# Other rows of a down-projection weight loaded apart, with 8 in place of 5 as the outermost dimension

## The chip, the cores and the metric

The kernel runs on one core of one Trainium2 chip. The metric is the time of one launch on the device in microseconds. Before the change it is 199.98 us (median of three runs, 199.91 to 200.15). A core has TensorE (PE; its weight loads are shown apart as PEld), VectorE (DVE), ScalarE (ACT), GpSimd (POOL) and SyncE (SP). Sixteen DMA engines move data between the chip's memory and the core's own memory, whose tiles have up to 128 partitions (rows) each.

## The reference

One token for each of 8 sequences passes a layer norm, then two branches that share the normalised `xn`, and the branches are multiplied:

```python
xn = _layernorm(x, axis=-1)                       # x: 8 x 1 x 512
s = _A_ref(xn, k_cache, v_cache, wq, wo)          # attention
g = _silu(_B_ref(xn, w_gate, w_up, w_down))       # gated unit
return x + s * g

# _A_ref: 32 query heads of 128, 8 key/value heads, the last 2048 of 8192 cached positions
# _B_ref:
g = xn @ w_gate; u = xn @ w_up                    # 512 x 1792 each
return (sigmoid(g) * u) @ w_down                  # 1792 x 512
```

All tensors are bf16. The caches are most of the traffic: the window of each sequence is 4 MB of keys and 4 MB of values, 67 MB in all. The weights wq, wo, w_gate, w_up and w_down add 4, 4, 1.75, 1.75 and 1.75 MB.

## The kernel before

Almost every load is issued from SP's queue (`q0`), in an order written out by hand: `later` puts a load on a list, and `pump` issues from the head of the list as long as the load's pool has a free buffer. There are two pools of large buffers, "k" with five and "v" with four; `free` gives a buffer back when its reader is done, and pumps. The order is: x and w_gate, w_up, the larger part of w_down, wq in two loads, the rest of w_down (`want_part`), then for 8 sequences x 2 halves of the heads a K tile and, three places later, a V tile of 2 MB each, and at last wo in five loads of 12, 8, 6, 4 and 2 rows per partition. SP carries out its instructions in order, so a load that has to wait for a buffer or for a semaphore holds up all that are behind it. Loads take turns on eight semaphores, and a load on a semaphore waits until the load before it on that semaphore has completed.

The work goes in this order. The layer norm and the transposes of `xn`; `hidden` (L291) multiplies by w_gate and w_up, with four column blocks of 448 side by side in the partitions of one PSUM tile; a sigmoid (L308), a product (L312) and a 32 x 32 block transpose on DVE (L320) give `hT_sb`, the hidden values with one of 14 rows per partition in each slice. The down projection (L348) multiplies slice by slice with the rows of w_down and ends in the gate `gg_sb` (L375). Then q (L385), and for each sequence the K tiles are transposed on TensorE (L481), copied (L486) and multiplied with q (L500); a softmax on ACT (L548); transposes of the weights (L571); the product with V (L597). The last lines multiply by wo (L719, L733), by the gate (L748) and add x (L750).

w_down has 1792 rows of 1 KB, 14 to a partition. Rows 1 to 13 of each partition are one load of 128 partitions (`wd_sb`, 13 KB per partition). Row 0 of all 128 partitions, 128 KB, goes elsewhere: `want_part` (L179) clears a tile of 64 partitions x 3 slots on POOL and fills it with three loads, whose source has an outermost dimension of 5, 5 and 4:

```python
PARTS = ((0, NA, 0, SX, 0, A), (Z, NA, 0, SX, SX * NA, A))     # A = 5, NA = 20, SX = 3, Z = 32
PARTS += ((Z + NA, P - 2 * SX * NA, 0, 1, 2 * SX * NA, 4),)
...
in_=src.rearrange("(y a) n -> a y n", a=a)[:, :, : SD * w.shape[1]],
```

As these rows lie in other partitions than the hidden values that belong to them, the kernel shifts the hidden values too: `sel_part` (L276 to L285), a 0/1 matrix made with seven copies, three matmuls (L327) and a copy (L335) put slice 0 of `hT_sb` into the partitions of `wd_part`. The down projection then is 13 matmuls with `wd_sb` and three with `wd_part`.

Of the kernel before, what the change touches and what calls it, by code (L numbers as in the profile page):

```python
# [10 lines left out]
def kernel(  # L11
# [13 lines left out]
    nc = tc.nc  # L25
    P = 128
    B, _, D = A_x.shape
    _, Hkv, Sk, Dh = A_k_cache.shape
# [3 lines left out]
    F = B_w_gate.shape[1]  # L32
    KT = D // P
    FT = F // P
# [14 lines left out]
    bf16 = mybir.dt.bfloat16  # L49
    f32 = mybir.dt.float32  # L50
    AF = mybir.ActivationFunctionType
    ALU = mybir.AluOpType
# [6 lines left out]
    vpool = ctx.enter_context(tc.tile_pool(name="vpool", bufs=4))  # L59
    ktpool = ctx.enter_context(tc.tile_pool(name="ktpool", bufs=3))  # L60
    ppool = ctx.enter_context(tc.tile_pool(name="ppool", bufs=2))
    consts = ctx.enter_context(tc.tile_pool(name="consts", bufs=1))
    work = ctx.enter_context(tc.tile_pool(name="work", bufs=1))
    small = ctx.enter_context(tc.tile_pool(name="small", bufs=2))
    ps_t = ctx.enter_context(
        tc.tile_pool(name="ps_t", bufs=4, space=bass.MemoryType.PSUM)
    )
# [13 lines left out]
    q0, q1 = nc.sync, nc.scalar  # L81
# [22 lines left out]
    weights = {}  # L104
    todo = []

    def later(tag, f):
        todo.append((tag, f))
# [7 lines left out]
    def free(tag):  # L116
        room[tag] += 1
        pump()

    def want_rows(name, w, tag, per, r0, r1):  # L120
        def f():
            t = load_rows(w, tag, per, r0, r1, name)
            for r in range(r0, r1):
                weights[(name, r)] = t[:, r - r0, :]

        later(tag, f)
# [13 lines left out]
    Z = 32  # L140
    S = Z // B
    NB = D // P
# [24 lines left out]

    A = 5  # L170
    SD = 1
    SX = 3
    HP = P // 2
    NA = 4 * A
    PARTS = ((0, NA, 0, SX, 0, A), (Z, NA, 0, SX, SX * NA, A))
    PARTS += ((Z + NA, P - 2 * SX * NA, 0, 1, 2 * SX * NA, 4),)
    d_room = []

    def want_part(w, per):  # L179
        def f():  # L180
            d = vpool.tile([HP, SX, SD, w.shape[1]], bf16, name="wd_part", tag="v")
            d_room.append(d)
            nc.gpsimd.memset(d[:], 0.0)
            for p0, n, x0, x1, s0, a in PARTS:
                m = n * (x1 - x0)
                src = w.rearrange("(y r) n -> y (r n)", r=per)[s0 : s0 + m]
                q0.dma_start(
                    out=d[p0 : p0 + n, x0:x1].rearrange("p x r n -> p (x r n)"),
                    in_=src.rearrange("(y a) n -> a y n", a=a)[:, :, : SD * w.shape[1]],
                )  # L190

        later("v", f)

    want_rows("wd_sb", B_w_down, "v", FT, SD, FT)
    for i in range(2):
        want_rows("wq_sb", A_wq, "k", KT, 2 * i, 2 * i + 2)
    want_part(B_w_down, FT)
    order = [(b, i) for b in range(B) for i in range(NQ)]
    AHEAD = 3
    for n in range(len(order) + AHEAD):  # L200
# [4 lines left out]
    for t0, t1 in ((0, 12), (12, KS), (KS, 26), (26, 30), (30, RT)):  # L205
# [4 lines left out]
    ident = consts.tile([P, P], bf16, name="ident")  # L210
# [6 lines left out]
        out=perm[:].rearrange("k (l p) -> k l p", l=G),  # L217
        in_=ident[:].rearrange("k (p l) -> k l p", l=G),
# [13 lines left out]
        out=rstd[:], in_=mv[:, 1:2], func=AF.Sqrt, bias=eps_t[:], scale=1.0  # L232
# [4 lines left out]
        out=xn_bf[:],  # L237
        in0=x_f[:],
# [7 lines left out]
    for kt in range(KT):  # L246
        nc.tensor.transpose(  # L247
            out=xnT_ps[:, kt, :],
            in_=xn_bf[:].rearrange("b (p kt) -> b kt p", kt=KT)[:, kt, :],
            identity=ident[:B, :B],  # L250
        )
    xnT_sb = work.tile([P, KT, Z], bf16, name="xnT_sb")
# [8 lines left out]
    for t in p_buf:  # L261
# [7 lines left out]
        out=own_q[:], in_=ident_f[:].rearrange("k (h q) -> k q h", q=NDQ), axis=AX.X  # L269
# [3 lines left out]
        out=sel_z[:], in_=ident_f[:].rearrange("k (j z) -> k z j", z=Z), axis=AX.X  # L273
    )

    sel_part = consts.tile([P, SX, HP], bf16, name="sel_part")  # L276
    nc.vector.memzero(sel_part[:])
    for p0, n, x0, x1, s0, a in PARTS:
        for x in range(x0, x1):
            nc.vector.tensor_copy(  # L280
                out=sel_part[:, x, p0 : p0 + n].rearrange("k (a e) -> k a e", a=a),
                in_=ident[:, s0 : s0 + n * (x1 - x0)].rearrange(
                    "k (e x a) -> k x a e", x=x1 - x0, a=a
                )[:, x - x0],
            )  # L285

    FC = F // NB

    def hidden(name):  # L291
        ps = ps_t.tile([P, FC], f32, name="h_ps", tag="t")
        for kt in range(KT):
            for j in range(NB):
                nc.tensor.matmul(  # L295
                    ps[Z * j : Z * (j + 1), :],
                    lhsT=xnT_sb[:, kt, :],
                    rhs=weights[(name, kt)][:, j * FC : (j + 1) * FC],
                    start=(kt == 0),
                    stop=(kt == KT - 1),  # L300
                    tile_position=(0, Z * j),
                    skip_group_check=True,
                )
        return ps

    g_ps = hidden("wg_sb")
    sig = ktpool.tile([P, CU * P // 2], f32, name="sig", tag="kT")
    nc.scalar.activation(out=sig[:, :FC], in_=g_ps[:], func=AF.Sigmoid)  # L308
    free("v")
    u_ps = hidden("wu_sb")  # L310
    h_sb = work.tile([P, FT, Z], bf16, name="h_sb")
    nc.vector.tensor_tensor(  # L312
        out=h_sb[:].rearrange("k t p -> k p t"),
        in0=sig[:, :FC].rearrange("k (p t) -> k p t", t=FT),
        in1=u_ps[:].rearrange("k (p t) -> k p t", t=FT),
        op=ALU.mult,
    )
    free("v")
    hT_sb = work.tile([P, FT, Z], bf16, name="hT_sb")
    nc.vector.transpose(  # L320
        out=hT_sb[:].rearrange("k t z -> k (t z)"),
        in_=h_sb[:].rearrange("k t p -> k (t p)"),
    )

    hP_ps = ps_t.tile([HP, SX, SD * Z], f32, name="hP_ps", tag="t")
    for x in range(SX):
        nc.tensor.matmul(  # L327
            hP_ps[:, x, :],
            lhsT=sel_part[:, x, :],
            rhs=hT_sb[:, :SD, :].rearrange("p t z -> p (t z)"),  # L330
            start=True,
            stop=True,
        )
    hP_sb = work.tile([HP, SX, SD * Z], bf16, name="hP_sb")
    nc.vector.tensor_copy(out=hP_sb[:], in_=hP_ps[:])  # L335
    down = [(hT_sb[:, t, :], weights[("wd_sb", t)]) for t in range(SD, FT)]
    for x in range(SX):
        top = max(p0 + n for p0, n, x0, x1, _, _ in PARTS if x0 <= x < x1)
        down += [
            (hP_sb[:top, x, Z * r : Z * (r + 1)], d_room[0][:top, x, r, :])  # L340
            for r in range(SD)
        ]


    w_ps = ps_s.tile([P, D], f32, name="w_ps", tag="s")
    for t, (h, w) in enumerate(down):
        j = t % NB
        nc.tensor.matmul(  # L348
            w_ps[Z * j : Z * (j + 1), :],
            lhsT=h,  # L350
            rhs=w,
            start=(t < NB),
            stop=(t >= len(down) - NB),
            tile_position=(0, Z * j),
            skip_group_check=True,
# [4 lines left out]
    for j in range(NB):  # L360
        nc.tensor.matmul(  # L361
            b_ps[Z * j : Z * (j + 1), :],
            lhsT=sel_z[:],
            rhs=w_sb[:, 0, j * P : (j + 1) * P],
            start=True,
            stop=True,
            tile_position=(0, Z * j),
            skip_group_check=True,
        )
    sigb = work.tile([P, P], f32, name="sigb")  # L370
    nc.scalar.activation(out=sigb[:], in_=b_ps[:], func=AF.Sigmoid)  # L371
    free("v")
    free("v")
    gg_sb = work.tile([P, P], f32, name="gg_sb")
    nc.vector.tensor_tensor(out=gg_sb[:], in0=sigb[:], in1=b_ps[:], op=ALU.mult)  # L375
# [5 lines left out]
    for kt in range(KT):  # L381
        for x in range(Hkv // JQ):
            for j in range(JQ):
# [3 lines left out]
                    lhsT=xnT_sb[:, kt, :],  # L387
                    rhs=weights[("wq_sb", kt)][:, g * rep * Dh : (g + 1) * rep * Dh],
                    start=(kt == 0),
                    stop=(kt == KT - 1),  # L390
                    tile_position=(0, Z * j),
                    skip_group_check=True,
# [3 lines left out]
    for x in range(Hkv // JQ):  # L396
        src = q_ps[x][:].rearrange("k (r d) -> k r d", r=rep)
# [4 lines left out]
    for x in range(Hkv // JQ):  # L402
        for r in range(rep):
            nc.tensor.transpose(  # L404
                out=qT_ps[:, x, r, :], in_=q_bf[:, x, r, :], identity=ident[:]
            )
        nc.vector.tensor_copy(
            out=qm_sb[:, :, x * JQ : (x + 1) * JQ, M0 : M0 + rep],
            in_=qT_ps[:, x].rearrange("d r (j z) -> d z j r", z=Z)[:, ::S],
# [11 lines left out]
    for i in range(NQ):  # L421
        nc.vector.tensor_copy(
            out=turn_rows[:].rearrange("k (i j l r) -> k i j l r", i=NQ, j=NJ, l=G)[
                :, i
            ],
            in_=ident[:].rearrange("k (l j i r) -> k i j l r", i=NQ, j=NJ, l=G)[:, i],
        )
        nc.vector.reduce_sum(
            out=sel_den[:, i * Hh : (i + 1) * Hh].rearrange("k (l r) -> k l r", l=G),
            in_=ident_f[:].rearrange("k (l j i r) -> k i l r j", l=G, j=NJ, i=NQ)[:, i],  # L430
            axis=AX.X,
        )
    for e in range(2):
        nc.vector.reduce_sum(
            out=sel_out[:, e, :].rearrange("k (i h) -> k i h", i=NQ),
            in_=ident_f[:].rearrange(
                "k (i m e h) -> k e i h m", i=NQ, m=NJ // 2, e=2
            )[:, e],
# [9 lines left out]
        out=sel_res[:],  # L448
        in0=sel_out[:, 0, :].unsqueeze(2).to_broadcast([P, Hq, NDQ]),
        in1=sel_out[:, 1, :].unsqueeze(2).to_broadcast([P, Hq, NDQ]),  # L450
        op=ALU.add,
# [3 lines left out]
        out=sel_sum[:], in_=sel_den[:].unsqueeze(2).to_broadcast([P, Hq, NDQ])  # L455
# [261 lines left out]
    for t in range(KS):  # L717
        j = t % NB
# [69 lines left out]
```

## Time and profile before

| what | value |
|---|---|
| time, median of 3 runs | 199.98 us (199.91 to 200.15) |
| profiled execution, span from first to last instruction | 198.0 us |
| around the span (199.98 - 198.0) | 2.0 us |
| PE, DVE, ACT busy in the span | 155.6, 122.6, 37.7 us |
| bytes read from memory | 81.02 MB, 409 GB/s over the span |
| last load's landing, start of the stores | 193.74 us, 194.87 us |

The page gives the busy time of each engine, a row of 40 slices of the span with the busy share of the DMA engines in tenths, and the queues with the share of the sixteen engines' time that their packets took. q1 is SP's queue, q10 is ACT's; q8 and q14 bring instructions. The waits list who stood idle and what ended it: "PE w_ps L348 <- DMA wd_part" is time in which the matmul of line 348 waited for that load, followed by the sum, the number of times and the longest. In the timeline, a bracket holds the idle time before an instruction and what ended it. The trace behind the page also holds every DMA packet with its start, length, size and queue, and the time of every semaphore update.

### The profile page before, as it was taken

What the parts mean: (1) busy time and instruction counts of PE and PEld (TensorE: products, weight loads), DVE (VectorE), ACT (ScalarE), POOL (GpSimd) and SP (SyncE); (2) the same over time, 40 slices, a digit from 0 to 9 for tenths busy, and PEclk for the clock granted to TensorE, in tenths of its full rate; (3) what the DMA queues carried; (4) which work ended last, traced back from release to release, by engine and by line L of the source; (5) the groups of instructions that cost most, each with busy time, mean ns of one, the idle gap of its engine ahead of it and who ended that gap; (6) DMA issues with size and microseconds to landing.
All of it is one profiled execution on the core that took longest, in us unless ns stands there. A gap on an engine that the chain in (4) does not pass through costs nothing.

```text
span 198.0 us, 4774 instructions
## 1 busy us (share of the span) xinstructions
PE 155.6 (79%) x2133; PEld 105.6 (53%) x2133; DVE 122.6 (62%) x234; ACT 37.7 (19%) x91; POOL 2.7 (1%) x11
## 2 busy tenths in 40 slices
PE   0434038999979999999798869996999997888552
PEld 0111014877766677656565646674667665566421
DVE  3773001999978679758675927686767874852301
ACT  3300011000620520150024000600060033082010
POOL 5000000000000000000000000000000000000000
PEclk9999999999999999999999979997899999999985
DMA  6999999999999999999999999999999999999980
GB/s 209 446 430 434 426 425 427 434 440 429 424 420 430 430 427 437 430 430 420 430 427 425 427 440 430 422 434 424 424 430 440 420 430 437 427 420 425 420 336 10
DMA packets 6441, 81.32 MB, mean 411 GB/s; under 512 B 782, under 2 KB 918, under 8 KB 1558
## 3 DMA queue, kind: packets, MB, share of 16 engines
q1 hardware_dynamic: 6224, 80.10, 95.0%
q10 hardware_dynamic: 198, 0.93, 1.4%
q8 instruction: 16, 0.26, 0.5%
q14 instruction: 3, 0.02, 0.0%
HBM read 81.02 MB, written 0.01 MB: 409 GB/s over the span
## 4 chain that ended last, share of the span: by engine, by line
DMA 57%; PE 36%; ACT 3%; DVE 1%; SPq 1%; issue 1%
DMA k_sb<-in_A_k_cache_dram 32%; PE kT_ps L481 19%; DMA wo_sb<-in_A_wo_dram 11%; DMA wd_part<-in_B_w_down_dram 10%; PE o_ps L597 6%; PE s_ps L500 5%; DMA wg_sb<-in_B_w_gate_dram 3%; ACT p_buf L548 2%; PE pT_ps L571 2%; PE q_ps L385 1%; SPq L99 1%; ACT L548 1%; PE qT_ps L404 1%; PE fin_ps L733 1%; PE b_ps L361 0%
## 5 line engine op out<-in xcount | busy, mean ns | idle before, releaser
L486 DVE COPY kT_sb<-kT_ps 128x1024 bf16<-128x1024 bf16 x128 | 85.4, 687 | 30.2 <-PE kT_ps L481 29.5
L481 PE MATMUL kT_ps<-perm,k_sb 128*128 128x128 bf16 x1024 | 78.0, 225 | 8.2 <-DMA k_sb<-in_A_k_cache_dram 8.2
L481 PEld LDWEIGHTS <-k_sb 128*128 128x128 bf16 x1024 | 61.1, 101 | 28.0 <-issue 16.7
L597 PE MATMUL o_ps<-v_sb,pT_sb 128*32 128x256 bf16 x512 | 40.3, 279 | 1.2 <-DVE o_sb L618 0.9
L597 PEld LDWEIGHTS <-pT_sb 128*32 128x32 bf16 x512 | 22.1, 97 | 10.3 <-issue 3.8
L500 PE MATMUL s_ps<-kT_sb,qm_sb 128*32 128x512 bf16 x256 | 26.0, 396 | 0.7 <-DVE kT_sb L486 0.7
L548 ACT ACTIVATE p_buf<-s_ps,nb 32x512 bf16<-32x512 f32 x32 | 21.8, 680 | 0.5
L541 ACT COPY nb<-m_ps 128x1 f32<-128x1 f32 x8 | 1.3, 160 | 88.3 <-PE m_ps L535 88.3
L571 PE MATMUL pT_ps<-turn_rows,p_buf 128*128 128x128 bf16 x128 | 11.0, 230 | 1.5 <-ACT p_buf L548 1.5
L564 DVE COPY pT_sb<-pT_ps 128x1024 bf16<-128x1024 bf16 x14 | 9.6, 687 | 3.9 <-PE pT_ps L571 3.9
L571 PEld LDWEIGHTS <-p_buf 128*128 128x128 bf16 x128 | 9.4, 151 | 3.4 <-ACT p_buf L548 2.1
L500 PEld LDWEIGHTS <-qm_sb 128*32 128x32 bf16 x256 | 6.6, 93 | 7.7 <-issue 1.4
L613 ACT ACTIVATE o_odd<-o_ps,own_col 128x128 f32<-128x128 f32 x8 | 2.9, 368 | 26.8 <-PE o_ps L597 26.7
L375 DVE TENSOR_TENSOR gg_sb<-sigb,b_ps 128x128 f32<-128x128 f32 x1 | 0.3, 289 | 12.2 <-ACT sigb L371 12.2
L348 PE MATMUL w_ps<-wd_part,hP_sb 52*32 52x512 bf16 (+1 forms) x3 | 0.6, 597 | 8.3 <-DMA wd_part<-in_B_w_down_dram 8.3
L548 ACT ACTIVATION_READ_ACCUMULATOR p_buf<-s_ps,nb 32x1 f32 x32 | 5.9, 184 | 0.0
L515 DVE TENSOR_REDUCE st<-s_ps 128x1 f32<-128x512 f32 x8 | 5.5, 682 | 0.5 <-PE s_ps L500 0.5
L348 PEld LDWEIGHTS <-hP_sb 52*32 52x32 bf16 (+1 forms) x3 | 0.1, 98 | 9.2 <-issue 9.2
L247 PE MATMUL xnT_ps<-ident,xn_bf 8*128 8x8 bf16 x4 | 0.3, 174 | 5.8 <-DVE xn_bf L236 5.8
L640 DVE SCALAR_TENSOR_TENSOR own<-m_ps,inv,own_q 128x128 f32<-128x128 f32 x8 | 2.8, 345 | 3.1 <-PE m_ps L631 3.1
L618 DVE SCALAR_TENSOR_TENSOR o_sb<-o_ps,own_col,o_odd 128x128 f32<-128x128 f32 x8 | 2.7, 341 | 3.1 <-ACT o_odd L613 3.1
L295 PE MATMUL h_ps<-wu_sb,xnT_sb 128*32 128x448 bf16 x16 | 1.7, 572 | 3.4 <-DMA wu_sb<-in_B_w_up_dram 3.4
(80 smaller groups left out, 67.1 us busy)
## 6 DMA issues: line engine op xcount, KB each, us to landing
k_sb<-in_A_k_cache_dram SPq DMA_DIRECT2D x16, 2048.0 KB, 29.9
v_sb<-in_A_v_cache_dram SPq DMA_DIRECT2D x16, 2048.0 KB, 27.2
wq_sb<-in_A_wq_dram SPq DMA_DIRECT2D x2, 2048.0 KB, 19.9
wu_sb<-in_B_w_up_dram SPq DMA_DIRECT2D x1, 1792.0 KB, 10.3
wd_sb<-in_B_w_down_dram SPq DMA_DIRECT2D x1, 1664.0 KB, 13.8
wo_sb<-in_A_wo_dram SPq DMA_DIRECT2D x1, 1536.0 KB
wo_sb<-in_A_wo_dram SPq DMA_DIRECT2D x1, 1024.0 KB, 20.1
wg_sb<-in_B_w_gate_dram ACTq DMA_DIRECT2D x1, 896.0 KB
```

The source lines that it names most:

```text
L99: q0.dma_start(out=t[:], in_=w.rearrange("(p r) n -> p r n", r=per)[:, r0:r1, :])
L481: nc.tensor.transpose(out=kT_ps[:, c, :], in_=k_sb[:, j * CU + h * CH + c, :], identity=perm[:],)
L486: nc.vector.tensor_copy(out=kT[(b, u)][:, h * CH : (h + 1) * CH, :], in_=kT_ps[:])
L500: nc.tensor.matmul(s_ps[b][NR * l : NR * (l + 1), :], lhsT=qm_sb[:, b, i * G + l, o : o + Z], rhs=t[:, :, PG * l : PG * (l + 1)], start=(u ...
L515: nc.vector.reduce_max(out=st[b][:], in_=s_ps[b][:], axis=AX.X)
L548: nc.scalar.activation(out=p_buf[b % 2][rows, :, l, :], in_=s[rows, :].rearrange("k (c p) -> k p c", p=PG), func=AF.Exp, bias=nb[rows, :], ...
L564: copy(out=pT[b][:, h * CH : (h + 1) * CH, :], in_=pT_ps.pop(h)[:])
L571: nc.tensor.transpose(out=pT_ps[h][:, c, :], in_=p_buf[b % 2][:, :, :, h * CH + c].rearrange("k p l -> k (p l)"), identity=turn_rows[:],)
L597: nc.tensor.matmul(o_ps[rows, b % 2, :].rearrange("k (e d) -> k e d", e=2), lhsT=pT[b][:, c, rows], rhs=v[:, m, c], start=(c == 0), stop=( ...
L613: nc.scalar.mul(out=o_odd[:], in_=o_ps[:, b % 2, Dh:], mul=own_col[:, 1:2])
L618: nc.vector.scalar_tensor_tensor(out=o_of[b // 2][:, b % 2, :], in0=o_ps[:, b % 2, :Dh], scalar=own_col[:, 0:1], in1=o_odd[:], op0=ALU.mul ...
L640: nc.vector.scalar_tensor_tensor(out=own[:], in0=m_ps[:, b % 2, P : 2 * P].rearrange("p (q t) -> p q t", q=NDQ), scalar=inv[y][:, b % 2 : ...
```

## The change

All 128 partitions now hold 12 rows of w_down each (rows 0 to 1535), one load of 12 KB per partition. The last 256 rows go, four to a partition, into partitions 0 to 63 of the same tile, in slots 12 to 15, with two loads of 32 partitions. Their source is written with 8 as its outermost dimension and 4 as the next, so that destination partition 4 a + p takes its 4 KB from block 8 p + a. All three loads are issued one after another, ahead of wq. The separate tile, its memset, its place in the "v" pool, `sel_part`, the three shifting matmuls and their copy are gone.

The hidden values are now computed where they are needed: `hidden` multiplies, beside four column blocks of 384 for the first 12 rows, two blocks of 128 for the last four, into the same PSUM tile; sigmoid, product and transpose are each done in two pieces, one over 128 partitions and one over 64. The down projection has 12 matmuls over 128 partitions and four over 64.

```diff
-    A = 5
-    SD = 1
-    SX = 3
     HP = P // 2
-    NA = 4 * A
-    PARTS = ((0, NA, 0, SX, 0, A), (Z, NA, 0, SX, SX * NA, A))
-    PARTS += ((Z + NA, P - 2 * SX * NA, 0, 1, 2 * SX * NA, 4),)
-    d_room = []
-
-    def want_part(w, per):
-        def f():
-            d = vpool.tile([HP, SX, SD, w.shape[1]], bf16, name="wd_part", tag="v")
-            d_room.append(d)
-            nc.gpsimd.memset(d[:], 0.0)
-            for p0, n, x0, x1, s0, a in PARTS:
...
-        later("v", f)
-
-    want_rows("wd_sb", B_w_down, "v", FT, SD, FT)
+    F0 = FT - 2
+    FX = 4
+    FR = F0 + FX
+    NE = 8
+
+    def want_down():
+        t = vpool.tile([P, FR, D], bf16, name="wd_sb", tag="v")
+        q0.dma_start(
+            out=t[:, :F0, :],
+            in_=B_w_down[: P * F0].rearrange("(p r) n -> p r n", r=F0),
+        )
+        for j in range(HP // Z):
+            f0 = P * F0 + j * Z * FX
+            q0.dma_start(
+                out=t[j * Z : (j + 1) * Z, F0:, :].rearrange("p r n -> p (r n)"),
+                in_=B_w_down[f0 : f0 + Z * FX].rearrange(
+                    "(p a r) n -> a p (r n)", a=NE, r=FX
+                ),
+            )
+        for r in range(FR):
+            weights[("wd_sb", r)] = t[:, r, :] if r < F0 else t[:HP, r, :]
+
+    later("v", want_down)
     for i in range(2):
         want_rows("wq_sb", A_wq, "k", KT, 2 * i, 2 * i + 2)
-    want_part(B_w_down, FT)
...
-    sel_part = consts.tile([P, SX, HP], bf16, name="sel_part")
...
-    FC = F // NB
+    FC = Z * F0
+    FE = Z * FX
...
+                w = weights[(name, kt)]
+                cols = [(0, FC, j * FC)]
+                if j < HP // Z:
+                    cols.append((FC, FE, NB * FC + j * FE))
+                for at, n, f0 in cols:
+                    nc.tensor.matmul(
+                        ps[Z * j : Z * (j + 1), at : at + n],
+                        lhsT=xnT_sb[:, kt, :],
+                        rhs=w[:, f0 : f0 + n],
...
-    nc.scalar.activation(out=sig[:, :FC], in_=g_ps[:], func=AF.Sigmoid)
+    h_parts = ((P, 0, FC), (HP, FC, FC + FE))
+    for n, f0, f1 in h_parts:
+        nc.scalar.activation(out=sig[:n, f0:f1], in_=g_ps[:n, f0:f1], func=AF.Sigmoid)
...
+    nc.vector.tensor_tensor(
+        out=h_sb[:HP, F0:, :].rearrange("k t (a p) -> k p a t", a=NE),
+        in0=sig[:HP, FC : FC + FE].rearrange("k (p a t) -> k p a t", a=NE, t=FX),
+        in1=u_ps[:HP, FC : FC + FE].rearrange("k (p a t) -> k p a t", a=NE, t=FX),
+        op=ALU.mult,
+    )
...
-    hP_ps = ps_t.tile([HP, SX, SD * Z], f32, name="hP_ps", tag="t")
...
-    hP_sb = work.tile([HP, SX, SD * Z], bf16, name="hP_sb")
-    nc.vector.tensor_copy(out=hP_sb[:], in_=hP_ps[:])
...
+    for n, t0, t1 in ((P, 0, F0), (HP, F0, FR)):
+        nc.vector.transpose(
+            out=hT_sb[:n, t0:t1, :].rearrange("k t z -> k (t z)"),
+            in_=h_sb[:n, t0:t1, :].rearrange("k t p -> k (t p)"),
+        )
+    down = [
+        (hT_sb[: P if t < F0 else HP, t, :], weights[("wd_sb", t)]) for t in range(FR)
+    ]
...
     nc.scalar.activation(out=sigb[:], in_=b_ps[:], func=AF.Sigmoid)
-    free("v")
     free("v")
```

More of the change, by code (lines that the diff above doesn't have):

```diff
@@ L165 @@
     want_rows("wu_sb", B_w_up, "v", KT, 0, KT)
-    A = 5
-    SD = 1
-    SX = 3
     HP = P // 2
-    NA = 4 * A
-    PARTS = ((0, NA, 0, SX, 0, A), (Z, NA, 0, SX, SX * NA, A))
-    PARTS += ((Z + NA, P - 2 * SX * NA, 0, 1, 2 * SX * NA, 4),)
-    d_room = []
-    def want_part(w, per):
-        def f():
-            d = vpool.tile([HP, SX, SD, w.shape[1]], bf16, name="wd_part", tag="v")
-            d_room.append(d)
-            nc.gpsimd.memset(d[:], 0.0)
-            for p0, n, x0, x1, s0, a in PARTS:
[L185 to L190, printed above, removed]
-        later("v", f)
-    want_rows("wd_sb", B_w_down, "v", FT, SD, FT)
+    F0 = FT - 2
[19 more added lines that the diff above has]
+    later("v", want_down)
     for i in range(2):
         want_rows("wq_sb", A_wq, "k", KT, 2 * i, 2 * i + 2)
-    want_part(B_w_down, FT)
     order = [(b, i) for b in range(B) for i in range(NQ)]
@@ L274 @@
     )
-    sel_part = consts.tile([P, SX, HP], bf16, name="sel_part")
[L277 to L285, printed above, removed]
-    FC = F // NB
+    FC = Z * F0
+    FE = Z * FX
     def hidden(name):
-        ps = ps_t.tile([P, FC], f32, name="h_ps", tag="t")
+        ps = ps_t.tile([P, FC + FE], f32, name="h_ps", tag="t")
         for kt in range(KT):
             for j in range(NB):
[L295 to L303, printed above, removed]
+                w = weights[(name, kt)]
[7 more added lines that the diff above has]
+                        rhs=w[:, f0 : f0 + n],
+                        start=(kt == 0 and at == 0),
+                        stop=(kt == KT - 1),
+                        tile_position=(0, Z * j),
+                        skip_group_check=True,
+                    )
         return ps
@@ L307 @@
     sig = ktpool.tile([P, CU * P // 2], f32, name="sig", tag="kT")
-    nc.scalar.activation(out=sig[:, :FC], in_=g_ps[:], func=AF.Sigmoid)
+    h_parts = ((P, 0, FC), (HP, FC, FC + FE))
+    for n, f0, f1 in h_parts:
+        nc.scalar.activation(out=sig[:n, f0:f1], in_=g_ps[:n, f0:f1], func=AF.Sigmoid)
     free("v")
     u_ps = hidden("wu_sb")
-    h_sb = work.tile([P, FT, Z], bf16, name="h_sb")
+    h_sb = work.tile([P, FR, Z], bf16, name="h_sb")
+    hT_sb = work.tile([P, FR, Z], bf16, name="hT_sb")
     nc.vector.tensor_tensor(
-        out=h_sb[:].rearrange("k t p -> k p t"),
-        in0=sig[:, :FC].rearrange("k (p t) -> k p t", t=FT),
-        in1=u_ps[:].rearrange("k (p t) -> k p t", t=FT),
+        out=h_sb[:, :F0, :].rearrange("k t p -> k p t"),
+        in0=sig[:, :FC].rearrange("k (p t) -> k p t", t=F0),
+        in1=u_ps[:, :FC].rearrange("k (p t) -> k p t", t=F0),
+        op=ALU.mult,
[4 more added lines that the diff above has]
+        in1=u_ps[:HP, FC : FC + FE].rearrange("k (p a t) -> k p a t", a=NE, t=FX),
         op=ALU.mult,
@@ L318 @@
     free("v")
[L319 to L323, printed above, removed]
-    hP_ps = ps_t.tile([HP, SX, SD * Z], f32, name="hP_ps", tag="t")
[L326 to L332, printed above, removed]
-        )
-    hP_sb = work.tile([HP, SX, SD * Z], bf16, name="hP_sb")
-    nc.vector.tensor_copy(out=hP_sb[:], in_=hP_ps[:])
[L336 to L342, printed above, removed]
+    for n, t0, t1 in ((P, 0, F0), (HP, F0, FR)):
+        nc.vector.transpose(
+            out=hT_sb[:n, t0:t1, :].rearrange("k t z -> k (t z)"),
+            in_=h_sb[:n, t0:t1, :].rearrange("k t p -> k (t p)"),
+        )
+    down = [
+        (hT_sb[: P if t < F0 else HP, t, :], weights[("wd_sb", t)]) for t in range(FR)
+    ]
     w_ps = ps_s.tile([P, D], f32, name="w_ps", tag="s")
```

## The prediction

> **What bounds the kernel now.** I read the DMA rows of the page first, because the slices of that row never fall.
>
> ```profile
> span 198.0 us, 4774 instructions
> ...
> DMA  6999999999999999999999999999999999999980
> ...
> DMA packets 6441, 81.32 MB, mean 411 GB/s; under 512 B 782, under 2 KB 918, under 8 KB 1558
> ## 3 DMA queue, kind: packets, MB, share of 16 engines
> q1 hardware_dynamic: 6224, 80.10, 95.0%
> ...
> q8 instruction: 16, 0.26, 0.5%
> q14 instruction: 3, 0.02, 0.0%
> ```
>
> The reader is to see that the queue of SP alone fills 95.0% of sixteen DMA engines' time, and that instruction queues (q8, q14) use the same engines. Next the end of the timeline, and the last step of the chain of waits in order of time:
>
> ```profile
> 190.12 0.62 PE L719 MATMUL part_ps<-wo_sb,oP_sb 128*32 128x512 bf16 x8 [1.21 <-DMA wo_sb<-in_A_wo_dram]
> ...
> 193.17 1.01 PE L733 MATMUL fin_ps<-wo_sb,oP_sb 128*32 128x128 bf16 x24 [0.39 <-DMA wo_sb<-in_A_wo_dram]
> ...
> 194.23 0.29 DVE L748 TENSOR_TENSOR prod<-gg_sb,fin_ps 128x128 f32<-128x128 f32 x1 [6.20 <-PE fin_ps L733]
> ```
>
> ```profile
> 170.90 22.23 DMA wo_sb<-in_A_wo_dram
> 193.17 1.04 PE fin_ps L733 x23
> ```
>
> TensorE stands waiting for rows of wo that were issued 22 us before: the end is the landing of the last load (193.74 by its last semaphore update), plus a fixed 4.3 us. Last, the stage of the change:
>
> ```profile
> PE w_ps L348 <- DMA wd_part<-in_B_w_down_dram: 8.3, 1, 8.3
> ...
> SPq L187 <- DMA wg_sb<-in_B_w_gate_dram: 1.7, 2, 1.3
> ```
>
> ```profile
> L187 SPq DMA_DIRECT2D wd_part<-in_B_w_down_dram x3: 675/752/974, 5.4 to 7.6; - x3
> ```
>
> The 8.3 us wait looks like the prize. It is not: a core that is bound by its DMA engines cannot finish sooner because TensorE starts sooner.
>
> **The sixteen engines, one by one.** The trace keeps each DMA packet's start, length, size and queue, but not its engine. On a busy engine a packet starts 3 or 4 ns before the last one's recorded end (a 16 KB packet is recorded as 611 ns and the next starts after 607), so packets can be joined into chains. From 8.5 us to the end all join into sixteen chains without a gap over 40 ns. So every engine is busy all the time at one pace, and the kernel ends with the engine that has most to do. From an engine's first wu packet to its last packet:
> - three engines have nothing extra: 183.40 us; they end at 189.98, 190.29, 190.50.
> - eight have two 16 KB instruction fetches of q8 each: 186.23. A fetch costs its engine (186.23 - 183.40)/2 = 1.42 us. They end at 193.00, 193.15, 193.24, 193.27, 193.35, 193.35, 193.38, 193.40, and these set the end.
> - five have the 1 KB packets of wd_part (24 of them: 184.43). They end at 190.89, 191.70, 191.84, and, with one and two 8 KB fetches of q14, 192.18 and 193.05.
>
> So the old load put its lump on five engines that have no q8 fetch. The question is which eight engines the new lump meets. A load's completions show how many engines it used: the two 20-partition parts (5 outermost) gave five updates each, the third (4) four, x_bf (8 partitions) eight, a 128-partition load sixteen. The eight of x_bf are a sample of "8 outermost". Followed from their 1 KB packets at 1.7 to 2.9 us, they are the five with wd_part, one with nothing extra (ends 189.98), and two with fetches: the one ending at 193.24 (joined packet to packet) and the one ending at 193.15 (joined only by order: the five engines that finish x_bf first are taken for the five that start wg first). By that, at least one engine that is already among the latest gets more.
>
> **The change part by part.** *Loads of w_down.* Packets of 13 KB come every 494 ns, of 12 KB (first wo load) every 456.5, of 4 KB (wo rows 26 to 30) every 155.3, of 1 KB every 42.5; a completion takes 6. Per engine:
> - before, all: 8 x 494 = 3.95; on four of the five 26 x 42.5 more (5.08 with completions), on the fifth 24 (4.99).
> - after, all: 8 x 456.5 = 3.65; on the eight also 8 x 155.3 (two loads, 4 partitions each): 4.91.
> - so the five change by -0.17 to -0.08, the other three of the eight by +0.95, the remaining eight by -0.30.
>
> New ends: 193.24 + 0.95 = 194.19; 193.15 + 0.95 = 194.11; the remaining fetch engines 193.40 - 0.30 = 193.10. The latest end moves from 193.40 to 194.19: **+0.8 us**, all on the path. Bounds: if a 4 KB packet into 64 partitions goes like four of 1 KB (170 ns), +0.12; the engines' starting offsets (first wu packets spread over 6.46 to 7.30) may shift this by 0.2 either way. The wo row is the nearest, so 0.8 stands, with 0.6 to 1.1 as ends.
>
> [...] By an even spread instead, the sum would be +0.3 (rival 2). [...]
>
> *SP.* Three issues with 2.86 us from 5.44 on go, and two come (0.4 to 0.6 each by the rows of SP) ahead of wq. SP's loads take turns on eight semaphores, so wq's first load now waits for wg (landed 5.36, 7.61) and queues wq and K behind it till then. The engines are in wu and wd until 15.9, so it is hidden with 8 us to spare; if not, engines idle by as much. Later semaphores shift by one place; the K tiles' issues still wait for L481 (124.6 us in sum), with some 20 us of loads queued.
>
> *POOL, DVE, ACT, PE.* The wd_part memset (1.38 at 0.87) goes, as do the memset and seven copies of sel_part (0.14 + 0.74), three L327 matmuls and the L335 cast (0.25); nothing waited for them but the down projection. Added: 16 matmuls of 128 columns (0.08 each by L361's eight in 0.66: 1.3), a second sigmoid (0.28 by L371), a second multiply (0.29 by L375 to 0.59 by a share of L312's 2.08), a second transpose (0.2 of 0.65). Together at most 2.5 us, in part beside each other, between 7.6 and 20 us; cover: TensorE waits there for wu (3.4) and then for wq, which lands near 26.5 (25.6 before, plus the 0.95 of parts now ahead of it). Zero; without the cover, up to 2 us. Down matmuls stay 16.
>
> *What is late next.* Without the wait for wd_part, q follows wq and K transposes may start near 30 in place of 34.46, but the first K tile lands near 31.4 (31.55 before). TensorE then waits for K. The gain of 3 us is slack.
>
> **Sum.** Span 198.0 + 0.8 = 198.8; around the span lie 199.98 - 198.0 = 2.0 us, so 200.78, against the median of 199.98 (199.91 to 200.15).
>
> **Rivals.** (1) *The eight engines hold no q8 fetch* (my joining at the start is wrong). Then the fetch engines all lose 0.30 and end at 193.10; the others end at 191.45 or before, the one with two q14 fetches at 192.9: 199.68, not slower. It decides if neither engine at 193.15 and 193.24 is among the eight. For it: the early packets overlap, one join is by order only. Against: the other is exact. (2) *The load spreads over sixteen*, not doing what its outermost 8 says: 12 + 2 rows on each, 3.65 + 4 x 155 = 4.28, so +0.32 on the latest: 200.3. Against: the 5, 5, 4. (3) *A third fetch on one of the two*: TensorE has 26 instructions more; +1.42: 202.2. Against: a fetch comes every 258 or so recorded instructions, the last at 4069, the program then ends at about 4300, before the next at 4327. (4) *TensorE's lag sets the end* and the 3 us come in: 197.0. For: the 8.3 us wait. Against: the chains without gaps, wo issued 22 us early.
>
> **How the numbers follow.** Forecast 0.67, rival 1 0.14, 2 0.06, 3 0.08, 4 0.05. The forecast's own range is 200.55 to 201.1. The range is 199.6 to 201.4: it takes in rivals 1 and 2 and leaves out 3 and 4 and a little of the tails. Two tenths of a per cent, 0.4 us, is about what a measurement of this kernel can tell from no change. Faster: rival 4 and the lower edge of 1, 0.08. Same: the rest of 1, 2 and the lowest of the forecast, 0.18. Slower 0.74.
>
> **What would show it.** Right: the two new loads complete on eight engines each; the latest engine end near 194.2 and only one or two engines there, the other fetch engines near 193.1; L348 without its 8.3 us wait, K transposes starting at 31 to 32 and waiting for k_sb. Wrong: latest ends near 193.1 in all fetch engines (rival 1), sixteen completions (rival 2), 17 fetches (3), or TensorE not waiting for wo at the end (4).

## The result and the profile after

| | before | after |
|---|---|---|
| median, nine runs each | 200.04 us (199.83 to 200.17) | 200.45 us (200.32 to 200.62) |
| ratio, 95% interval | | 1.0020 (1.0012 to 1.0029) |
| profiled execution: span, time | 198.0, 199.98 us | 198.8, 200.62 us |

The changed kernel is slower by 0.41 us in the medians and by 0.64 us between the two profiled executions. The forecast was 200.78, a rise of 0.80; the medians rose by half of that. Of all executions told of below one, of the load on four engines, took 204.59 us beside five of 200.23 to 200.85, and is left out of the median. First the page of the kernel after, in the parts that were shown of before:

```profile
span 198.8 us, 4791 instructions
...
DMA  6999999999999999999999999999999999999960
...
DMA packets 6380, 81.33 MB, mean 409 GB/s; under 512 B 784, under 2 KB 792, under 8 KB 1496
## 3 DMA queue, kind: packets, MB, share of 16 engines
q1 hardware_dynamic: 6162, 80.10, 94.5%
...
q8 instruction: 17, 0.28, 0.5%
q14 instruction: 3, 0.02, 0.0%
```

The same 80.10 MB come in 62 packets fewer, and the slices are as full as before up to the last but one, which fell from 8 to 6: more engines have ended by then, though the last one ends later. Then the end of the timeline and of the chain of waits:

```profile
191.01 0.61 PE L703 MATMUL part_ps<-wo_sb,oP_sb 128*32 128x512 bf16 x8 [1.16 <-DMA wo_sb<-in_A_wo_dram]
...
194.12 1.04 PE L717 MATMUL fin_ps<-wo_sb,oP_sb 128*32 128x128 bf16 x24 [0.43 <-DMA wo_sb<-in_A_wo_dram]
...
195.21 0.29 DVE L732 TENSOR_TENSOR prod<-gg_sb,fin_ps 128x128 f32<-128x128 f32 x1 [6.24 <-PE fin_ps L717]
```

```profile
171.92 22.16 DMA wo_sb<-in_A_wo_dram
194.12 0.62 PE fin_ps L717 x15
194.76 0.43 PE fin_ps L717 x8
```

The last matmuls again wait for wo; their start moved from 193.17 to 194.12, the product from 194.23 to 195.21. The stage of the change, TensorE's timeline before:

```profile
16.78 1.89 PE L348 MATMUL w_ps<-wd_sb,hT_sb 128*32 128x512 bf16 x13
26.99 0.61 PE L348 MATMUL w_ps<-wd_part,hP_sb 60*32 60x512 bf16 x3 [8.32 <-DMA wd_part<-in_B_w_down_dram]
...
34.46 1.81 PE L481 MATMUL kT_ps<-perm,k_sb 128*128 128x128 bf16 x15
```

and after:

```profile
16.82 2.02 PE L333 MATMUL w_ps<-wd_sb,hT_sb 128*32 128x512 bf16 x16 [2.94 <-DVE hT_sb L321]
...
21.61 1.90 PE L369 MATMUL q_ps<-wq_sb,xnT_sb 128*32 128x512 bf16 x16 [1.43 <-DMA wq_sb<-in_A_wq_dram]
26.48 1.90 PE L369 MATMUL q_ps<-wq_sb,xnT_sb 128*32 128x512 bf16 x16 [2.97 <-DMA wq_sb<-in_A_wq_dram]
...
31.34 3.46 PE L465 MATMUL kT_ps<-perm,k_sb 128*128 128x128 bf16 x32 [1.13 <-DMA k_sb<-in_A_k_cache_dram]
```

All sixteen down matmuls run in one stretch, the 8.3 us wait is gone, and the K transposes start at 31.34 in place of 34.46, now waiting for the K tile. Those 3 us did not reach the end.

Joining the packets of the trace into sixteen engines as in the prediction gives, from an engine's first w_up packet to its last packet (us). A lump is what an engine gets of the small loads; the two engines with a lump and 8 KB fetches of q14 are left out:

| what the engine has | before | after |
|---|---|---|
| nothing extra | 183.40 | 183.10 |
| two 16 KB instruction fetches (q8) | 186.23, eight engines | 185.93, six |
| lump of w_down, no fetch | 184.43 to 184.54 | 184.35 to 184.38 |
| lump and two q8 fetches | none | 187.19 and 187.26, two |
| last packet ends, latest engines | 193.40 | 194.29 and 194.37 |

Each of the two small loads has eight semaphore updates, the first from 15.65 to 16.08 us, the second from 16.29 to 16.71, and every 4 KB packet is recorded with 159 ns. So the new lump lies on eight engines, and two of these hold fetches.

### The profile page after: what moved, and what is told of

The parts are those of the page before. It is cut to its first block, busy times and chain, and to the rows that moved or that the text cites. A ratio compares the mean times of both kernels' runs of the same rounds, so it can differ in the third digit from the quotient of the medians.

```text
span 198.8 us, 4791 instructions
## 1 busy us (share of the span) xinstructions
PE 154.6 (78%) x2146; PEld 105.0 (53%) x2146; DVE 121.9 (61%) x227; ACT 37.7 (19%) x92; POOL 1.4 (1%) x10
## 3 DMA queue, kind: packets, MB, share of 16 engines
q1 hardware_dynamic: 6162, 80.10, 94.5%
## 4 chain that ended last, share of the span: by engine, by line
DMA 78%; PE 17%; SPq 1%; DVE 1%; issue 0%
DMA k_sb<-in_A_k_cache_dram 64%; DMA wo_sb<-in_A_wo_dram 11%; PE kT_ps L465 11%; DMA wg_sb<-in_B_w_gate_dram 3%; PE s_ps L484 3%; PE o_ps L581 2%; SPq L99 1%; PE pT_ps L555 1%; PE fin_ps L717 1%; DVE st L499 0%; DVE kT_sb L470 0%; SPq L149 0%; DVE prod L732 0%; DVE y_bf L734 0%; PE m_ps L502 0%
## 5 line engine op out<-in xcount | busy, mean ns | idle before, releaser
L465 PE MATMUL kT_ps<-perm,k_sb 128*128 128x128 bf16 x1024 | 77.2, 224 | 14.6 <-DMA k_sb<-in_A_k_cache_dram 14.6
L465 PEld LDWEIGHTS <-k_sb 128*128 128x128 bf16 x1024 | 60.4, 100 | 34.9 <-DMA k_sb<-in_A_k_cache_dram 18.3
L581 PE MATMUL o_ps<-v_sb,pT_sb 128*32 128x256 bf16 x512 | 39.8, 277 | 1.1 <-DVE o_sb L602 0.9
L369 PE MATMUL q_ps<-wq_sb,xnT_sb 128*32 128x512 bf16 x32 | 3.8, 627 | 4.4 <-DMA wq_sb<-in_A_wq_dram 4.4
L287 PEld LDWEIGHTS <-xnT_sb 128*32 128x32 bf16 x48 | 2.1, 125 | 6.1 <-issue 5.0
L385 DVE CAST q_bf<-q_ps 128x512 bf16<-128x512 f32 x1 | 0.7, 691 | 7.6 <-PE q_ps L369 7.6
L369 PEld LDWEIGHTS <-xnT_sb 128*32 128x32 bf16 x32 | 1.1, 130 | 6.6 <-issue 4.8
L287 PE MATMUL h_ps<-wu_sb,xnT_sb 128*32 128x384 bf16 (+1 forms) x24 | 1.9, 451 | 3.2 <-DMA wu_sb<-in_B_w_up_dram 3.2
```

The source lines that it names most:

```text
L287: nc.tensor.matmul(ps[Z * j : Z * (j + 1), at : at + n], lhsT=xnT_sb[:, kt, :], rhs=w[:, f0 : f0 + n], start=(kt == 0 and at == 0), stop=( ...
L369: nc.tensor.matmul(q_ps[x][Z * j : Z * (j + 1), :], lhsT=xnT_sb[:, kt, :], rhs=weights[("wq_sb", kt)][:, g * rep * Dh : (g + 1) * rep * Dh ...
L465: nc.tensor.transpose(out=kT_ps[:, c, :], in_=k_sb[:, j * CU + h * CH + c, :], identity=perm[:],)
L581: nc.tensor.matmul(o_ps[rows, b % 2, :].rearrange("k (e d) -> k e d", e=2), lhsT=pT[b][:, c, rows], rhs=v[:, m, c], start=(c == 0), stop=( ...
```

## The experiments

Times are medians beside runs of the kernel before on the same chip. "Work" is the time from an engine's first w_up packet to its last packet, "start" when that first packet began.

**TensorE's early wait alone.** The kernel before with its small loads ahead of wq, as the new ones are.

```diff
+    want_part(B_w_down, FT)
     for i in range(2):
         want_rows("wq_sb", A_wq, "k", KT, 2 * i, 2 * i + 2)
-    want_part(B_w_down, FT)
```

> The kernel before with the loads of its separate rows issued ahead of wq in place of behind it, nothing else. TensorE's 8.3 us wait at the down projection goes, K transposes start near 31.4 in place of 34.5. Theory: the bytes of each engine are unchanged, so the end is too: 0.0 within 0.15 us. Rival (TensorE's lag counts): up to 3 us faster.

Measured: 199.78 against 199.78, ratio 1.0000 (0.9991 to 1.0009). That is what the theory expected. In TensorE's timeline of this kernel the wait for `wd_part` is gone and the transposes start earlier by 2.6 us:

```profile
18.82 0.61 PE L348 MATMUL w_ps<-wd_part,hP_sb 60*32 60x512 bf16 x3
...
31.86 3.60 PE L481 MATMUL kT_ps<-perm,k_sb 128*128 128x128 bf16 x32 [1.16 <-DMA k_sb<-in_A_k_cache_dram]
```

The wait was slack; rival 4 falls, and the change of place of the loads costs nothing either.

**Other counts of engines.** Sixteen in place of eight; then half the rows (13 rows for all, two more on 64 partitions) on eight engines and on four. All three leave the destination partitions as they are; if each outermost index has an engine of its own (the loads with 8 outermost had eight updates each), an engine writes two neighbouring partitions of each 32 with sixteen outermost, and eight with four.

```diff
-    NE = 8
+    NE = 16
```

> The changed kernel with 16 in place of 8 as the outermost dimension of the two small loads, nothing else. Theory (the DMA engine with most to do sets the end): the two loads complete on sixteen engines, each engine gets 3.65 + 4 x 0.155 + 0.01 = 4.28 us of w_down rows. Against the changed kernel's profile the two late engines (194.29, 194.37) lose 0.63 and the other engines with two instruction fetches (up to 193.31) gain 0.63, so all eight end between 193.5 and 193.95, and the time is about 0.4 us below the changed kernel's and 0.3 us above the kernel before. Rival (the added matmuls, sigmoid and multiply or the order of the loads made it slower, not the engines): same time as the changed kernel, 200.45.

```diff
-    F0 = FT - 2
-    FX = 4
+    F0 = FT - 1
+    FX = 2
```

> The changed kernel with 13 rows per partition for all and two more on partitions 0 to 63, still 8 outermost: half the lump, on the same eight engines. Theory: every engine has 3.95 for 13 rows, the eight 8 packets of 2 KB at 0.080 more, 4.6 in all; the two of the eight with fetches end 0.64 later than in the kernel before (193.15 + 0.64 and 193.24 + 0.64 = 193.9), the other fetch engines where they were (193.40): +0.5 against before by the packets, about half to all of it in the time. Rival: same as the changed kernel.

```diff
-    F0 = FT - 2
-    FX = 4
+    F0 = FT - 1
+    FX = 2
...
-    NE = 8
+    NE = 4
```

> As the one with half the lump, but with 4 as the outermost dimension. Theory: the lump goes to four engines that have no TensorE fetch (16 packets of 2 KB, 1.28: 5.24 against 5.08 before, so they stay below 193.3); the eight fetch engines have the same bytes as in the kernel before and end at 193.4 as there. Time as the kernel before within 0.15 us, though it computes with the changed kernel's instructions. Rival (instructions): slower than before by the same 0.4 as the changed kernel.

| kernel | time, us | ratio to before (199.78) | small packets | loss elsewhere |
|---|---|---|---|---|
| sixteen engines | 201.29 | 1.0069 (1.0057 to 1.0082) | 4 KB: 159 to 438 ns, median 311 | 0.4 to 1.3 us per engine before 30 us |
| half, eight engines | 200.05 | 1.0008 (0.9999 to 1.0017) | 2 KB: all 84 ns | none |
| half, four engines | 200.35 | 1.0029 (1.0017 to 1.0041) | 2 KB: 84, in the second load up to 139 ns | 0.57 us on engines without a lump |

The middle one went as the engine sums say: 186.87 and 186.97 of work on the two engines with lump and fetches, 186.23 on the others with fetches. Its time rose by 0.27, about half of the 0.5 of the packets, and the interval just takes in no change. The other two did not go as expected. With sixteen engines the time should have risen by 0.3; it rose by 1.5. With four engines, none of which holds a q8 fetch, the time should have stayed; it rose by 0.57. In both the packets themselves were slow, and while they ran so were other engines' packets of wq. The page shows it as a dip in the fourth slice (15 to 20 us) of the bytes moved. Kernel after, sixteen engines, half on four engines, in this order:

```profile
GB/s 205 441 423 440 428 432 428 425 432 424 438 425 428 428 428 428 432 425 432 432 419 437 428 435 420 432 425 432 425 428 438 425 428 428 428 425 430 412 277 9
```

```profile
GB/s 222 437 415 339 437 420 434 430 427 434 422 430 430 427 427 427 434 427 434 427 427 429 427 437 424 425 427 430 437 420 427 434 437 427 424 427 434 407 313 9
```

```profile
GB/s 213 441 432 378 429 429 433 439 426 426 421 426 433 436 429 426 426 423 420 446 433 431 423 423 426 434 436 429 429 420 429 426 439 429 433 423 436 399 346 16
```

440 GB/s there in the kernel after, 339 and 378 in these. So the count of engines and the bytes are not all; my second theory was that it matters which partitions an engine writes. The trace does not name engines. If they are numbered by the outermost index, the loads that ran at full speed (8 outermost over 32 partitions, 4 KB in 159 ns, and the two larger old ones, 5 over 20, 1 KB in 46 ns) give engine e the four partitions from 4e on, or from 32 + 4e; the loads with slow packets give it others. One load does not fit: the third small load of the kernel before, 8 KB on four engines into partitions 52 to 59, gives each engine partitions of others, and its 1 KB packets were recorded with the same 46 ns as the rest. So writing elsewhere does not cost in every case.

**Which partitions.** Two tests from both sides: the kernel after with its extra rows in partitions 64 to 127 and the hidden values for them there too, everything else equal; and four engines again, but each on its own four partitions (from 0 and from 32), with the same bytes as the slow load on four.

```diff
-                out=t[j * Z : (j + 1) * Z, F0:, :].rearrange("p r n -> p (r n)"),
+                out=t[HP + j * Z : HP + (j + 1) * Z, F0:, :].rearrange("p r n -> p (r n)"),
...
```

> The kernel after with its four more rows in partitions 64 to 127 in place of 0 to 63; bytes, packets, sizes and the outermost 8 are the same. Theory A (each engine has partitions that it reaches undisturbed: the first eight engines blocks of four partitions in the lower half, as the loads of 8 and of 5 outermost had them, the others blocks in the upper half): the first eight engines now write where the last eight write. The 4 KB packets take more than the 159 ns of the kernel after, up to twice as long, and the engines without a lump lose time too (as 0.57 us with the load of four engines); the time is 0.3 to 1.5 us above that of the kernel after, that is 0.7 to 1.9 above before. Theory B (only the number of engines and the bytes count): packets of 159 ns and the time of the kernel after, 0.4 above before. [...]

```diff
-    F0 = FT - 2
+    F0 = FT - 1
...
-    NE = 8
+    NE = 4
+    ZX = Z // 2
...
+        x = work.tile([HP, FX, D], bf16, name="wd_x")
...
-                out=t[j * Z : (j + 1) * Z, F0:, :].rearrange("p r n -> p (r n)"),
+                out=x[j * Z : j * Z + ZX].rearrange("p r n -> p (r n)"),
...
```

> As the load on four engines, but each engine's rows lie in its own block of four partitions in both halves of the first 64: 128 rows of w_down, four to a partition, in partitions 0 to 15 and 32 to 47 of a tile of its own, two loads with 4 outermost; the other 13 rows of all partitions as before. Theory A (partitions of one's own): packets of 4 KB take 159 ns, no other engine loses time in its wq packets, and as the first four engines hold no fetch (5.2 us of w_down each, 1.25 more than the fetch engines, which need 2.8 for their fetches) the time is that of the kernel before within 0.15. Theory B (four engines are too few, wherever they write): slower packets and the 0.57 us of the earlier load on four engines again.

| kernel | time, us | ratio to before (200.00) | 4 KB packets |
|---|---|---|---|
| after, upper half | 201.63 | 1.0092 (1.0072 to 1.0112) | 159 to 328 ns, median 300 |
| four engines, own partitions | 199.91 | 1.0003 (0.9990 to 1.0016) | all 159 ns |

Both went as theory A said; that the last eight engines have blocks of their own in the upper half, no run shows. In the upper half engines without lump or fetch need 184.25 in place of 183.10, 1.15 more, in wq packets that start between 14.7 and 17.7 us. The two late engines need 188.34 and 188.44 and end at 195.23 and 195.25. The row of bytes dips once more:

```profile
GB/s 214 438 427 335 427 436 436 423 423 435 430 427 427 427 430 436 423 436 420 430 430 435 423 427 425 436 433 417 433 430 433 427 430 430 427 423 428 418 294 7
```

With own partitions the four engines keep full speed, the engines with fetches have their 186.23, and the time is that of before. This kernel computes with the two products and two sigmoids of the kernel after, so these pieces cost nothing either. The pair of the kernel after and its upper half shows that the place decides, at equal bytes, packet size and number of engines; the two loads on four engines agree, at equal bytes, but their packets differ in size too (2 KB and 4 KB). What jams inside was not measured.

**No lump at all.** The kernel before with all 14 rows of a partition in one load; the parts, the selection and the shifted values go.

```diff
-    want_rows("wd_sb", B_w_down, "v", FT, SD, FT)
+    want_rows("wd_sb", B_w_down, "v", FT, 0, FT)
...
-    want_part(B_w_down, FT)
...
```

> The kernel before with nothing loaded apart: all 14 rows of w_down in each partition, one load of 14 KB packets on sixteen engines, no shifted values. My theory (the engines that hold two instruction fetches set the end, and what counts is the bytes given to them): they go from eight packets of 13 KB (494 ns each) to eight of 14 KB (531 ns, the cadence of w_gate's and w_up's packets), 0.30 more, so the time is 0.3 us above that of the kernel before (0.1 to 0.5). There is only one load of 128 partitions, so no engine writes beside another one as in the loads of sixteen engines or of 8 neighbouring partitions above. Rival (moving rows off the fetch engines is worth nothing): the same time as before, within 0.1.

Measured: 200.39 against 200.00, ratio 1.0021 (1.0012 to 1.0030). The engines with two fetches need 186.53 in place of 186.23: the 0.30 forecast; the time rose by 0.39, within what was expected. The old load on five engines was worth this; the new one (200.39 in the next experiment) takes as long as having none.

**The kernel after again,** unchanged, for the size.

> The kernel after once more, beside the others on this chip. If the size of the change is what the result gave, 0.41 us above before (0.25 to 0.6); if the 0.8 us of the two profiles is nearer, 0.6 to 1.0. I expect 0.3 to 0.7, and that the starts of the two late engines (6.92 and 7.02 us before, 7.03 and 7.18 after in the profiles) differ again by 0.1 to 0.5 from those of the first profile.

Measured: 200.39 against 200.00, ratio 1.0030 (1.0016 to 1.0043), so 0.39, close to the first 0.41. Its profiled execution took 200.13, the lowest of its eleven; the one profiled first, 200.62, was the highest of its nine. The work on the engines is the same in both, the starts are not:

```
                      two late engines: start + work = end     the other six with fetches
after, 200.62 us      7.03 + 187.26 = 194.29                   last start 7.38, end 193.31
                      7.18 + 187.19 = 194.37
after again, 200.13   6.55 + 187.18 = 193.73                   last start 7.34, end 193.28
                      6.67 + 187.18 = 193.85
```

The latest ends differ by 0.52, the times by 0.49. This end is visible in the timeline of the second execution, where the product of L732 starts 0.49 earlier:

```profile
194.72 0.29 DVE L732 TENSOR_TENSOR prod<-gg_sb,fin_ps 128x128 f32<-128x128 f32 x1 [6.39 <-PE fin_ps L717]
```

**The fetches.** Both kernels with most of TensorE's instructions gone.

```diff
-        if h == 0:
+        if h == 0 and u in (0, NU - 1):
...
+        if u in (0, NU - 1):
+            turn(b, u, h, k_sb, j)
...
+        if 0 < u < NU - 1:
+            return
...
-            for m in range(NJ // 2):
+            for m in range(NJ // 2) if c in (0, CU - 1) else ():
```

> The kernel after with most of the attention's arithmetic left out: K transposes and scores only for the first and last unit of each sequence, V products only for the first and last of the column groups. All loads are kept, byte for byte. TensorE then has about a third of its instructions, so that 5 or 6 fetches of 16 KB come in place of 16, at most one to an engine. Theory (two fetches of 1.42 us on each of eight engines decide which engines end last): every engine of the two-fetch kind loses at least 1.42. The latest of after, 187.19 us of work, falls to 187.19 - 1.42 = 185.77 if one of the two engines with a lump keeps one fetch, to 184.36 if neither does. With starts of 6.5 to 7.4 the last load ends at 192.3 to 193.1, at the lowest 191.6, in place of 193.8 to 194.4, and the time is 0.8 to 2.5 us below that of the kernel before, provided that the work behind the last load keeps its 4.3 us. Rival (fetches are only beside the loads, the bytes set the end): the time of the kernel after, 0.4 above before.

> The kernel before with the same parts of the attention left out (K transposes and scores but for the first and last unit of each sequence, V products but for the first and last column groups), all loads kept. Theory: an engine with one fetch has 186.23 - 1.42 = 184.81 us of work, one with a lump and none 184.43 (with the fetches of VectorE up to 186.1); the last load ends at 192.0 to 192.6 and the time is 0.8 to 1.5 us below that of the kernel before. Beside the lean kernel after: without second fetches the new lump costs what the engine with a lump and a fetch has more than one with a fetch alone, 185.77 - 184.81 = 0.96, or nothing if neither of the two has one. Rival: the time of the kernel before.

Measured: 198.90, ratio 0.9955 (0.9938 to 0.9972), and 198.63, ratio 0.9941 (0.9927 to 0.9956), beside 199.78. The page of the lean kernel after, with the same bytes and six fetches:

```profile
span 197.1 us, 1836 instructions
...
PE 89.4 (45%) x738; PEld 58.3 (30%) x738; DVE 61.7 (31%) x131; ACT 37.7 (19%) x92; POOL 1.4 (1%) x10
...
DMA  6999999999999999999999999999999999999970
...
q1 hardware_dynamic: 6162, 80.10, 95.2%
...
q8 instruction: 6, 0.10, 0.2%
```

Its last two engines are the same two kinds, a lump and now one fetch each: 185.76 and 185.77 of work (forecast 185.77), ending at 192.60 and 192.61. In the lean kernel before an engine with one fetch has 184.81 to 184.85 (forecast 184.81), and the last end, 192.25, is that of an engine with a lump and one fetch of q14 (three of q14 here as before, with VectorE at 138 instructions in place of 234; whose instructions they bring is not shown). So TensorE's instructions are paid for by the DMA engines: against the full kernels the time falls by 1.15 before (199.78 - 198.63) and about 1.3 after (199.78 + 0.40 - 198.90). That TensorE has less to do does not explain it: it waits for wo at the end in the full kernels too, and the work of the DMA engines shrank by the 1.42 of a fetch, to 0.01 us on the two late engines of the kernel after (187.18 to 185.76 and 185.77).

No version that does all the work came out faster than the kernel before by more than 0.1 us. The engines with two fetches are already spared once. Sparing them twice, which was not run, would save 0.30 and put 256 rows on five engines, one of which has two q14 fetches and 186.05 already with the 32 rows of the kernel after. With some 51 rows it would by this estimate become the latest.

## Why the prediction was right, and where its size was off

- *The path.* Right. The DMA engines end the kernel, one by one; the 8.3 us wait was slack (the loads moved alone: 0.00).
- *Which engines.* Right, the point that decided the sign: eight engines, of which two hold fetches. The prediction had joined one of the two by order only, and that guess held as well. Rival 1 (no fetch among the eight) falls with the table of the result.
- *Cost per engine.* Right to 0.01 for most: -0.30 for the remaining engines (185.93 and 183.10), +0.95 for the late ones (187.18 and 187.19 against 186.23; one of the four measured 187.26), 156 ns for a 4 KB packet's share.
- *Latest end, +0.8 us.* Mis-sized, and this is the main step that made 200.78 out of 200.45. That the span after is 198.8 to the digit is luck: the latest end moved by 0.97 (193.40 to 194.37), not by 0.79, and the stretch behind it, which the prediction took as fixed, fell from 4.60 to 4.46 (from the end of the last packet to the end of the span). The term "starting offsets may shift this by 0.2 either way" was too small, and it had a sign. Before, the end is set by the last starter of eight engines with equal work; after, by the later of two. In the ten profiles of kernels with all their arithmetic the last start among the eight engines with two fetches is 7.11 to 7.63, mean 7.33; the later start of the two that are also among the first eight engines is 6.67 to 7.18, mean 6.94 (the five profiles in which they could be told). The 0.95 of work therefore becomes about 0.95 - 0.39 = 0.56 in the end on average, by this estimate, and 0.4 was measured. The rest is within the 0.5 by which two executions of the kernel after differ. The stretch from the end of the last packet to the end of the launch varies too: 6.58 in the profiled execution of before, 6.25 and 6.28 in the two of after, 6.18 to 6.88 over all kernels; why was not found.
- *Around the span, 2.0 us.* The first 199.98 - 198.0 was on the high side: the later runs of before have 1.73 to 1.75 in the medians, the profiled run after 200.62 - 198.8 = 1.8, all its runs 1.76 in the median. So of the 0.33 between forecast and median, 0.16 is from here (200.78 - 200.62); the other 0.17 (200.62 - 200.45) is by how much the profiled execution was above the median of its kernel. The forecast's own range, 200.55 to 201.1, lay too high by 0.1; the wide one held.
- *Edits at nothing.* Right in the sum, though not all in their rows. wq's second load ended TensorE's wait at 26.48 (forecast near 26.5), K at 31.34 (31.4). The second multiply took 0.91, above the 0.29 to 0.59 allowed. The down matmuls run behind it, from 16.82 to 18.84, but TensorE still waits 1.43 for wq ahead of 21.61:

```profile
L307 DVE TENSOR_TENSOR h_sb<-sig,h_ps 128x384 bf16<-128x384 f32 x1 | 1.8, 1822 | 3.3 <-PE h_ps L287 3.3
...
L313 DVE TENSOR_TENSOR h_sb<-sig,h_ps 64x128 bf16<-64x128 f32 x1 | 0.9, 914 | 0.0
```

- *Rival 2, +0.3.* Its condition was not met, and its price was wrong as well: sixteen engines on the same partitions cost 1.5, with slow packets, where the prediction had full speed. The tests on partitions make it likely that this is from the partitions that the engines write (4 KB packets of 300 ns in the median in the upper half, of 159 in the lower); how it comes about was not measured.
- *Rival 3, a third fetch.* The reading that the program ends before a 17th fetch was wrong: the kernel after has one (q8 17 above), but at 195.2 us, behind the last load, where it costs nothing.

The number of engines, eight, was read from the updates of loads in the trace of before (5, 5, 4 and 8 for as many outermost), and each new load had eight. Few engines cost nothing by themselves here: confined to four engines without fetches, each on its own partitions, the load left the time as it was (199.91 against 200.00), and five engines saved 0.39 against an even load; eight, two of them with fetches, took as long as the even load (200.39 each).

## What to carry to other kernels

When every DMA engine is busy from start to end, add up the work engine by engine, instruction fetches included, and give extra bytes only to engines that are not the latest. Choose the source's outermost dimension for the engines (5, 4 and 8 had as many updates here), and lay the destination so that each outermost index writes the four-partition blocks that the fast loads here gave it (4 KB in 159 ns, in the upper half in a median of 300); check a small load by the length of its packets and by a dip in the row of bytes. Where the end is a maximum over several engines, a profile pair says too much or too little by the scatter of their starts; take the size from many runs.

## What the runs showed of the hardware

- Two loads that gave the outermost indices other partitions than the fast loads (sixteen outermost; eight into the upper half) had their 4 KB packets about doubled (159 to a median of 311 and 300 ns). Engines without a lump or fetch lost 1.15 us beside the load into the other half, and engines without a lump 0.57 beside the load of 2 KB packets on four engines. No run here shows what held them up.
- A 16 KB instruction fetch cost its DMA engine 1.42 us (186.23 of work with two of them, 183.40 with none), more than twice the 0.607 of a 16 KB data packet, and the sixteen of q8 that came before the last load's end, in the kernel before and in the one after, went to only eight of the sixteen engines, two each. They go with TensorE's instructions: 16 and 17 in all at 2133 and 2146 matmuls, 5 and 6 at 725 and 738.
- The first w_up packets of the sixteen engines start over 0.6 to 1.05 us in the profiles (6.46 to 7.30 in that of before, 6.48 to 7.53 in that with early loads), and not in the same order each time: one of the two late engines is the first of all in the second profile of after (6.55) and not in the first (7.03). As the joined packets of an engine have no gap over 40 ns after 8.5 us (kernel before), the offset is carried to the end, 187 us later.
